# A sign test of 1024 hidden units, done for all of them or, after a bound over 24 token blocks, for the open ones alone

## The chip, the core and the metric

The kernel runs on one core of one Trainium2 chip. The metric is the device time of one execution in microseconds (us). A lower number is better. The chip's TensorE (PE) multiplies matrices, VectorE (DVE), ScalarE (ACT) and GpSimd (POOL) do elementwise work, and SyncE (SP) starts most transfers. Each works off its own list of instructions in order, and they wait for one another by semaphores.

## What is computed

Three layers follow each other. The first is windowed attention with block summaries on 4 x 8 heads of 768 tokens. The second is a soft mixture of experts: 3072 tokens are spread over 32 slots, 8 experts work on 4 slots each, and every token gets a weighted sum of the 32 slot outputs. The third is a top-1 mixture: each token goes through the one expert that its logits choose. Cut to what matters here:

```python
c = np.exp(logits - logits.max(1, keepdims=True))      # combine weights, 3072 x 32
c /= c.sum(1, keepdims=True) + 1e-09
x = c @ slot_out                                       # slot_out is 32 x 512
...
for e in range(E):                                     # 8 experts, top-1
    mask = expert_idx == e
    h = np.maximum(x[mask] @ w1[e], 0.0)               # 1024 hidden units
    out[mask] = gate_w[mask, None] * (h @ w2[e])
```

All tokens of an expert share `u = slot_out @ w1[e]`, which is 32 x 1024: the value of a hidden unit for a token is the product of 32 combine weights and a column of `u`.

## The kernel before

The kernel takes the expert of the first token, loads its weights, and treats all tokens by it first; a loop behind it treats the experts that are then still missing. Within that expert it uses that a unit whose value has the same sign for all tokens needs no `max`: it is zero for all of them or linear in `c`. The linear ones are summed into a 32 x 512 matrix. Only the mixed units have to be computed for each token; up to 96 are allowed (`NPL`), and with the 32 linear rows they fill 128 rows. If there are more, the code of the expert that is treated (`cbx`) becomes zero and the loop at the end does the expert's full product.

The program is in this order.

1. Attention, then the soft mixture (to about 187 us of the profile). Late in it the combine weights are transposed piece by piece into `cT` (`comb_pe`, `comb_ev`, L193 to L201): 128 rows that hold the weights' high and low parts twice, and 3072 columns, one for a token. `first_expert` (L795) chooses the expert and starts the loads of its weights `w1e` and `w2e`.
2. `g_half` and `g_sum` (L984, L998) multiply the slot outputs with `w1e` in two halves of 512 units and sum the parts; `g_parts` (L1001) splits the sum into the high and low rows of `G`. `tok` (L1094) computes logits and norms of the tokens, 128 tokens to a matmul.
3. The sign test: `tile_mm` and `tile_ev` (L1043, L1056), 24 tiles of 128 units by 1024 tokens. Each tile is two matmuls of 512 columns, and its maximum against the sign of the first token is taken while it is read out of PSUM, in turn by ACT and by DVE. Four PSUM areas of two banks are used in the order of the list `order`.
4. `rank` and `places` (L1140, L1168) number the mixed units, make one-hot matrices `OH` of the numbers, collect the columns of these units in `Gm` by matmuls, and fetch their rows of `w2` by an indirect DMA. `lin` (L1122) makes the linear part. Pieces of the norms and codes (`norms`, `codes`) are put between the tiles.
5. The end: `mixed` (L1266) computes the 128 rows for 512 tokens at a time, and 24 groups of three matmuls (L1291 to L1293) write the result `py` of 128 tokens each, which DVE and ACT scale by the gate, and SP writes out. `fill` and the matmuls named `warm` compute nothing that is used.

The order of the work on every engine is that of the code, since the schedule is written by hand; a wait stands where the data need it, and where a PSUM area is used again. In the sign test the main lines are:

```python
for i in range(3 * NU):
    tile_ev(i, tile_mm(i))
    ...
pf = dbank(1, "fill")
fill(6, pf)
rank(6, NU, pf)
places(6, NU, pf)
```

Of the kernel before, what the change touches and what calls it, by code (L numbers as in the profile page):

```python
# [22 lines left out]
P = 128  # L23
# [18 lines left out]
NPL = 96  # L42

# [91 lines left out]
def tile_kernel(ctx, tc, qT, kTd, vwd, phi, w1, w2, emb, tau, u1, u2, consts, consts2, out):  # L135
# [641 lines left out]
    cb = fp.tile([P, 1], F32, name="cb")  # L777
    w1e, w2e = [], []
# [43 lines left out]
    for r in range(2):  # L822
        for fc in range(8):
# [90 lines left out]
    def norms(i):  # L914

        if i == 0:
            for b in range(B):
# [90 lines left out]
    iota = con2[:, C_IOTA : C_IOTA + NPL]  # L1008
    pos = scr[:, 0, 120 : 128]
    ngs = scr[:, 0, 128 : 136]  # L1010
    us = fp.tile([P, NU, 2], F32R, name="us")
    GTf = scr[:, 2, 256:512].rearrange("p (k s) -> p k s", s=NSLOT)
    GNf = hx[:, 3, 256:512].rearrange("p (k s) -> p k s", s=NSLOT)
    GN = w2h[1][:, 0:2, :].rearrange("p a (k x) -> p (a k) x", x=P)
    acc = scr[:, 0, 152 : 176].rearrange("p (k j) -> p k j", j=3)
    fmx = scr[:, 0, 136 : 144]
    flag = fp.tile([P, NU + 1], BF16, name="flag")
    rk = scr[:, 0, 144 : 152]
    idx = fp.tile([P, 1], I32, name="idx")
    OH = w2h[0][:, 0:2, :].rearrange("p a x -> p (a x)")[:, 0 : NU * NPL].rearrange("p (k x) -> p k x", x=NPL)  # L1020
# [3 lines left out]
    junk = [hhi[0].rearrange("p a b -> p (a b)")[:, 0:1024], hlo[0].rearrange("p a b -> p (a b)")[:, 0:1024]]  # L1024
# [6 lines left out]
    with ExitStack() as es:  # L1031
        pst = es.enter_context(tc.tile_pool(name="pst", bufs=1, space=PSUM, reuse_waits="tile"))
        order = [0, 1, 0, 2, 1, 0, 2, 3, 1, 0, 2, 3] + [1, 2, 3] * 4
# [4 lines left out]
        def fill(n, ph):  # L1038

            for _ in range(n):  # L1040
                nc.tensor.matmul(ph[:, 0:512], cTt(0, P), cTt(0, 512), start=True, stop=True)

        def tile_mm(i):  # L1043
# [3 lines left out]
            for c in range(2):  # L1047
                nc.tensor.matmul(  # L1048
                    ph[:, c * 512 : c * 512 + 512],
                    G[:, k * P : (k + 1) * P],  # L1050
                    cTt(1024 * j + 512 * c, 512),
                    start=True,
                    stop=True,
# [3 lines left out]
        def tile_ev(i, ph):  # L1057

            k, j = divmod(i, 3)
            if i % 2 and i != 19:  # L1060
                nc.vector.tensor_tensor_reduce(  # L1061
                    out=junk[1],
                    in0=ph,
                    in1=ngs[:, k : k + 1].to_broadcast([P, 1024]),
                    scale=1.0,
                    scalar=0.0,
                    op0=ALU.mult,
                    op1=ALU.max,
                    accum_out=acc[:, k, j : j + 1],
                )  # L1070
            else:
                nc.scalar.activation(  # L1072
                    junk[0], ph, AF.Relu, scale=ngs[:, k : k + 1], accum_out=acc[:, k, j : j + 1]
                )
# [3 lines left out]
        nc.gpsimd.memset(flag, 0.0)  # L1078
        nc.gpsimd.tensor_copy(us, con2[:, C_U : C_U + NU].unsqueeze(2).to_broadcast([P, NU, 2]))
# [5 lines left out]
        def first(f):  # L1085
            ks = slice(4 * f, 4 * f + 4)
            for k in range(4 * f, 4 * f + 4):
                nc.tensor.matmul(ph0[:, k, :], G[:, k * P : (k + 1) * P], cTt(0, 2), start=True, stop=True)
            nc.vector.tensor_scalar(out=pos[:, ks], in0=ph0[:, ks, 0], scalar1=0.0, scalar2=None, op0=ALU.is_ge)
            nc.vector.tensor_scalar(  # L1090
                out=ngs[:, ks], in0=pos[:, ks], scalar1=-2.0, scalar2=1.0, op0=ALU.mult, op1=ALU.add
            )

# [4 lines left out]
        def kl():  # L1098
            nc.scalar.copy(KL, pk)
            nc.vector.tensor_tensor(out=KL[64:P], in0=pk[64:P], in1=KL[64:P].bitcast(F32), op=ALU.subtract)  # L1100

        def g_cols(k0, k1):
            for k in range(k0, k1):
                nc.tensor.matmul(
                    pgT[:, k, :], pgs[k // 4][:, (k % 4) * P : (k % 4) * P + P], sel[:, 0:NSLOT],
                    start=True, stop=True,
                )
# [4 lines left out]
        def halves(d, name):  # L1112
            t = dbank(d, name)
            return t[:, 0:512], t[:, 512:1024]

        def columns():
            nc.scalar.copy(GTf, pgT)
            nc.gpsimd.tensor_tensor(out=GPT, in0=GTf, in1=pos.unsqueeze(2).to_broadcast([P, NU, NSLOT]), op=ALU.mult)
            nc.gpsimd.tensor_tensor(out=GNf, in0=GTf, in1=ngs.unsqueeze(2).to_broadcast([P, NU, NSLOT]), op=ALU.mult)
            g2 = GNf.unsqueeze(2).to_broadcast([P, NU, 2, NSLOT])  # L1120
            g4 = GN.rearrange("p k (r c s) -> p k r c s", r=2, c=2)
            nc.gpsimd.tensor_copy(g4[:, :, 0], g2)  # L1122
            nc.gpsimd.tensor_tensor(out=g4[:, :, 1], in0=g2, in1=g4[:, :, 0].bitcast(F32), op=ALU.subtract)

# [265 lines left out]
```

## Time and profile before

| | us |
|---|---|
| Median of 3 runs | 259.67 (259.56 to 260.99) |
| Profiled execution | 260.86 |
| Its span, first to last instruction | 259.1 |
| PE busy in it | 236.1 (91%) |
| DVE, ACT, POOL busy | 149.9, 127.3, 91.8 |
| From the end of the slots' sum (187.65) to the first `phm` matmul | 39.9 |
| From there to the first `py` matmul | 4.4 |

The span is what the trace covers; the execution's own time lies 1.76 us above it, and 1.19 us above the median. Times of the trace are counted from the span's start. A matmul of 32-bit data is two records of the trace; PEld is the load of the weights that a matmul holds fixed, which runs beside the matmul before it. The clock column is the granted clock of TensorE: 1.00 is 2.4 GHz, 0.50 is 1.2 GHz, and a value between them is a stretch in which it changed.

### The profile page before, as it was taken

The numbers are of one execution on the slowest core, as the hardware profiler recorded it, in microseconds if no ns is written. First come the engines' busy times: TensorE is split into PE (matmuls) and PEld (weight loads), VectorE is DVE, ScalarE is ACT, GpSimd is POOL, SyncE is SP. The second block draws the span as 40 slices with busy tenths as digits, with TensorE's granted clock in tenths as the row PEclk, the third lists the DMA queues.
The fourth block names the chain that finished last, engine by engine and source line by source line (L and its number), as shares of the span: only waits on it lengthen the run. The fifth ranks groups of instructions, "written<-read, shape, count | busy, mean of one in ns | idle before, by whom it ended". The sixth has DMA issues, their size and how long they took to land.

```text
span 259.1 us, 7977 instructions
## 1 busy us (share of the span) xinstructions
PE 236.1 (91%) x3076; PEld 156.9 (61%) x3076; DVE 149.9 (58%) x697; ACT 127.3 (49%) x291; POOL 91.8 (35%) x131
## 2 busy tenths in 40 slices
PE   6688999989999999999999999998999997879980
PEld 2466877767767778677775433323656844547760
DVE  2547878758778778787855411342115476656840
ACT  1443765657647666467673121423226378434550
POOL 0256577556657665576640100000113540010000
PEclk9979999999999999999999999999999589967997
DMA  6999999999989999955799999997790000014892
GB/s 209 392 411 375 347 331 379 355 367 319 343 306 369 368 326 339 325 226 164 266 339 385 409 397 409 406 408 260 252 385 15 0 0 1 3 30 171 314 399 98
DMA packets 33658, 72.53 MB, mean 280 GB/s; under 512 B 2712, under 2 KB 4504, under 8 KB 33616
## 3 DMA queue, kind: packets, MB, share of 16 engines
q1 hardware_dynamic: 33552, 71.77, 76.0%
q8 instruction: 26, 0.43, 0.6%
q0 software_dynamic: 64, 0.20, 0.3%
q14 instruction: 16, 0.13, 0.1%
HBM read 65.67 MB, written 6.29 MB: 278 GB/s over the span
## 4 chain that ended last, share of the span: by engine, by line
PE 82%; DVE 6%; DMA 2%; issue 2%; ACT 2%; POOL 1%; SPq 1%; POOLq 0%; DVEq 0%; ACTq 0%
PE po L357 11%; PE pt L344 8%; PE s L302 8%; PE pO L831 6%; PE ph L755 6%; PE pv L250 5%; PE tx L390 5%; PE pht L1048 5%; PE lp L408 3%; PE py L1291 3%; DMA fix<-in_kT_dram 2%; PE py L1292 2%; PE pd L262 2%; PE py L1293 2%; PE pa L465 2%
## 5 line engine op out<-in xcount | busy, mean ns | idle before, releaser
L330 POOL TENSOR_TENSOR fix<-fix,nb 128x360 f32<-128x360 f32 x64 | 49.1, 789 | 50.8 <-DVE nb L317 50.6
L317 DVE CUSTOM_DVE_ANT_0 fix<-s,con 128x120 f32<-128x120 f32 x192 | 41.7, 278 | 18.1 <-PE s L302 16.1
L345 ACT COPY pts<-pt 120x384 f32<-120x384 f32 x64 | 27.7, 482 | 13.1 <-PE pt L344 13.1
L336 ACT ACTIVATE fix<-fix 128x360 f32<-128x360 f32 x64 | 29.2, 509 | 7.2 <-POOL fix L330 7.2
L357 PE MATMUL po<-vw,pts 120*64 120x65 f32 x768 | 30.4, 226 | 2.2 <-POOL vw L268 1.0
L357 PEld LDWEIGHTS po<-vw,pts 120*64 120x64 f32 x768 | 25.7, 138 | 8.3 <-issue 2.9
L344 PE MATMUL pt<-con,fix 128*120 128x128 f32 x192 | 28.0, 281 | 1.2 <-ACT fix L336 1.2
L268 POOL COPY vw<-vw 24x780 f32<-24x780 f32 x31 | 26.7, 861 | 2.0 <-POOL fix L330 0.2
L344 PEld LDWEIGHTS pt<-con,fix 128*120 128x120 f32 x192 | 21.4, 140 | 7.4 <-issue 5.0
L1061 DVE CUSTOM_DVE_ANT_0 hlo<-pht,scr 128x1024 fp32r<-128x1024 f32 x11 | 13.3, 1212 | 10.0 <-PE pht L1048 9.9
L374 DVE TENSOR_TENSOR X<-po,den 128x384 f32<-128x384 f32 x32 | 17.8, 557 | 1.1
L400 ACT COPY xT<-tx 128x384 f32<-128x384 f32 x32 | 15.3, 480 | 6.1 <-PE tx L390 5.2
L302 PE MATMUL s<-fix,fix 64*64 64x120 f32 x480 | 17.7, 271 | 0.6 <-DVE nb L317 0.4
L1048 PE MATMUL pht<-cT,gs 128*128 128x512 f32 x48 | 16.8, 478 | 0.6 <-ACT hhi L1072 0.4
L390 PE MATMUL tx<-con,X 128*128 128x128 f32 x96 | 16.4, 282 | 0.0
L1072 ACT ACTIVATE hhi<-pht,scr 128x1024 fp32r<-128x1024 f32 x13 | 14.5, 1116 | 3.9 <-PE pht L1048 3.7
L317 DVE DVE_READ_ACCUMULATOR2_ANT nb<- 128x1 f32 x192 | 16.0, 83 | 0.0
L831 PE MATMUL pO<-w,hx 128*32 128x512 f32 (+1 forms) x152 | 15.4, 509 | 0.0
L278 DVE TENSOR_REDUCE hm<-fix 128x48 f32<-128x768 f32 x16 | 15.1, 944 | 0.4 <-DMA fix<-in_kT_dram 0.4
L302 PEld LDWEIGHTS s<-fix,fix 64*64 64x64 f32 x480 | 12.6, 132 | 4.4 <-issue 3.1
L250 PE MATMUL pv<-vw,con 120*32 120x130 f32 x384 | 15.1, 287 | 0.1
L755 PE MATMUL ph<-w,siT 128*32 128x512 f32 x128 | 14.8, 596 | 0.4 <-DVE siT L578 0.4
(243 smaller groups left out, 356.6 us busy)
## 6 DMA issues: line engine op xcount, KB each, us to landing
w<-in_moe_w_dram SPq DMA_DIRECT2D x30, 1024.0 KB, 10.2
vw<-in_vw_dram SPq DMA_DIRECT2D x32, 390.0 KB, 6.8
fix<-in_kT_dram SPq DMA_DIRECT2D x15, 484.0 KB, 5.4
out_dram<-Y SPq DMA_DIRECT2D x24, 256.0 KB, 2.5
fix<-in_qT_dram SPq DMA_DIRECT2D x15, 384.0 KB, 5.9
w1e<-in_moe_w_dram SPq DMA_DIRECT2D x4, 512.0 KB, 4.4
w2e<-in_moe_w_dram SPq DMA_DIRECT2D x4, 512.0 KB, 8.9
wx<-in_moe_w_dram SPq DMA_DIRECT2D x1, 1024.0 KB, 10.8
```

What stands on the lines that cost most here:

```text
L250: nc.tensor.matmul(pv[32 * g : 32 * g + 32, 0:130], con[:KW, b0 : b0 + 32], vw[:KW, par, x0 : x0 + 130], start=c == 0, stop=c == 2,)
L302: nc.tensor.matmul(sp[j][64 * i : 64 * i + 64, c, :], qns[n % 3][64 * j : 64 * j + 64, 64 * t : 64 * t + 64], kTs[n % 3][64 * j : 64 * j + ...
L317: nc.vector.tensor_tensor_reduce(out=sms[u % 2][:, j, c, :], in0=sp[:, c, :], in1=con[:, m0 : m0 + KW], scale=-0.125, scalar=3.0e38, op0=A ...
L330: nc.gpsimd.tensor_tensor(out=sm, in0=sm, in1=st_["nb", u][:, j].unsqueeze(2).to_broadcast([P, 3, KW]), op=ALU.subtract)
L336: nc.scalar.activation(sm, sm, AF.Exp, scale=-1.0)
L344: nc.tensor.transpose(pt[:, c, :], sms[u % 2][:, j, c, :], ident)
L345: nc.scalar.copy(pts[:, j], pt)
L357: nc.tensor.matmul(po[64 * i : 64 * i + 64, c, j, :], pts[:, j, c, 64 * i : 64 * i + 64], vw[:KW, i, x0 : x0 + 65], start=True, stop=True,)
L390: nc.tensor.transpose(pt[:, c * P : c * P + P], st_["X", b][:, c0 + c, hp * P : hp * P + P], ident)
L755: nc.tensor.matmul(ph[32 * g : 32 * g + 32, :], siT[:, kc, :], w[:, g, :], start=kc == 0, stop=kc == 3)
L831: nc.tensor.matmul(po[c][32 * g : 32 * g + 32, 0 : cs.stop - cs.start], hTs[r][:, fc, 32 * g : 32 * g + 32], w[:, g, cs], start=(r, fc) in ...
L1048: nc.tensor.matmul(ph[:, c * 512 : c * 512 + 512], G[:, k * P : (k + 1) * P], cTt(1024 * j + 512 * c, 512), start=True, stop=True,)
```

## The change

The 24 exact tiles go. In their place there are two levels.

First a bound. The tokens are taken as 24 blocks of 128. While `cT` is made, DVE takes the maximum and the minimum of each of the 32 weights over each block (`box`, 16 reductions), and POOL makes of them a matrix `M` (`box_ends`): a block's midpoints and half widths, with a small slack. A unit's value in a block is at most midpoint times `u` plus half width times `|u|`, so one matmul for 128 units (`bounds`) gives the upper bounds of the unit and of its negative for all blocks, beside the unit's own column. A unit whose bounds leave one sign is settled. The others are called open.

Then the exact test on open units alone. They are numbered in each half of 512 units (`rank1`), at most 128 of a half are collected (`places1`, `candidates`), and 2 x 3 tiles are done as before. The mixed ones among them are numbered again (`rank2`) and collected (`mixed_units`). If a half has over 128 open units or over 96 units are mixed, the full product at the end does the expert (`fits`). The `fill` matmuls go; parts of norms and codes move behind the test.

```diff
+    def box(b, j, bx):
+        v = cTt(b * S, S).bitcast(F32).rearrange("p (g j t) -> p g j t", j=2, t=P)[0:96, :, j, :]
+        for w, op in enumerate((ALU.max, ALU.min)):
+            nc.vector.tensor_reduce(bx[:, w, 6 * b + 3 * j : 6 * b + 3 * j + 3], v, axis=AX.X, op=op)
...
+                late_box = 8 * r + fc in (C_STEPS[4], C_STEPS[5])
+                boxes.append((b, j))
+                if not late_box:
+                    for x in boxes:
+                        box(*x, bx)
+                    boxes.clear()
+                if (b, j) == (B - 1, 1):
+                    box_ends(bx, bm, M)
...
-        order = [0, 1, 0, 2, 1, 0, 2, 3, 1, 0, 2, 3] + [1, 2, 3] * 4
+        order = [1, 3, 2, 1, 3, 2]
...
+        def bound_rows(f):
+            g, pg, h = G[:, f * 512 : f * 512 + 512], pgb[f], slice(NSLOT, 2 * NSLOT)
+            nc.scalar.copy(g[0:64], pg[0:64])
+            nc.scalar.activation(g[64:96], pg[64:96], AF.Abs)
+            nc.vector.tensor_tensor(out=g[h], in0=pg[h], in1=g[h].bitcast(F32), op=ALU.subtract)
+
+        def bounds(f):
+            for k in range(4 * f, 4 * f + 4):
+                nc.tensor.matmul(pub[f][:, k % 4, :], G[0:96, k * P : (k + 1) * P], M, start=True, stop=True)
...
+        def rank1(f):
+            prk = prk1[:, 8 * f : 8 * f + 5]
+            nc.tensor.matmul(prk, ltb, flag1[:, f], start=True, stop=False)
+            for k in range(4):
+                nc.tensor.matmul(
+                    prk[:, k + 1 : 5], oneb, flag1[:, f, k : k + 1].to_broadcast([P, 4 - k]),
+                    start=False, stop=k == 3,
+                )
+
+        def places1(f):
+            ks = slice(4 * f, 4 * f + 4)
+            nc.vector.scalar_tensor_tensor(
+                out=rk[:, ks], in0=prk1[:, 8 * f : 8 * f + 4], scalar=1.0, in1=flag1[:, f, 0:4],
+                op0=ALU.add, op1=ALU.mult,
+            )
             for k in range(4 * f, 4 * f + 4):
...
+                nc.vector.tensor_scalar(
+                    out=OH1[:, k], in0=iota, scalar1=rk[:, k : k + 1], scalar2=ngs[:, k : k + 1],
+                    op0=ALU.is_equal, op1=ALU.mult,
+                )
...
-        for i in range(3 * NU):
-            tile_ev(i, tile_mm(i))
...
-        pf = dbank(1, "fill")
-        fill(6, pf)
-        rank(6, NU, pf)
-        places(6, NU, pf)
...
+        pgs = [g_half(f, A[:, 512 * f : 512 * f + 512]) for f in range(2)]
+        for f in range(2):
+            g_sum(pgs[f], pgb[f])
+        bound_rows(0)
+        bound_rows(1)
         for c in range(4):
             nc.tensor.matmul(pk, soT[:, c, :], SOE[:, c, P - NSLOT :], start=c == 0, stop=c == 3)
         kl()
...
+        bounds(0)
+        bounds(1)
+        flags(0)
+        flags(1)
+        columns(0)
+        columns(1)
+        prk1, pgc = halves(0, "rank1")
+        tok(0, 4)
+        rank1(0)
+        tok(4, 8)
+        rank1(1)
+        tok(8, 12)
         pl_out(0)
...
+        places1(0)
+        tok(12, 20)
+        candidates(0)
+        places1(1)
+        tok(20, 24)
+        pl_out(1)
+        candidates(1)
...
+        for i in range(6):
+            ph = tile_mm(i)
+            tile_ev(i, ph)
+            if i in (3, 5):
+                f = i // 4
+                p = candidates_t(f)
+                nc.scalar.copy(GNc[:, f], p)
+        prk2, pgm = halves(1, "rank2")
+        lin(0)
+        rank2(0)
+        rank2(1)
+        mixed_units()
+        norms(2)
+        fits(cbx, prk2[:, 2:3], NPL, cbs[:, 1:2])
```

Three places show how the instructions move. The first is TensorE behind the slots' sum, before the change: `L988` is `g_half`, `L999` is `g_sum`, `L1096` is `tok`, `L1088` is the sign of the first token, `L1048` are the exact tiles `pht`.

```order
L1211 MATMUL pre_3120<-hx 128x40 x4
L988 MATMUL pre_3118<-w1e_2988,hx 32x512 x2
L988 MATMUL pre_3118<-w1e_2989,hx 32x512 x2
L1096 MATMUL pre_3120<-KL,cT_2868 128x40 x6
L999 MATMUL pre_3119<-scr,con 128x512
L1096 MATMUL pre_3120<-KL,cT_2868 128x40 x6
L1041 MATMUL pre_3118<-cT_2868 128x512 x2
```

After the change the same stretch of TensorE reads so: both halves of `g_half` (`L1017`) and `g_sum` (`L1028`) come first, then `pk` (`L1256`) and the bounds (`L1113`), and `tok` (`L1184`) stands between the numbering (`L1150`) and the collecting of open units (`L1171`).

```order
L1028 MATMUL pre_3154<-scr,con 128x512
L1028 MATMUL pre_3154<-hx,con 128x512
L1256 MATMUL pre_3155<-hx 128x40 x4
L1113 MATMUL pre_3156<-M,gs 128x112 x8
L1184 MATMUL pre_3155<-KL,cT_2868 128x40 x4
L1150 LDWEIGHTS ltb
L1150 MATMUL rank_3208<-flag_3140,ltb 128x5
```

The numbering now follows four matmuls of `tok`, where the exact tiles had begun. A few rows further down TensorE's list goes on like this, up to the first of the tiles that are left.

```order
L1184 MATMUL pre_3155<-KL,cT_2869 128x40 x8
L1171 MATMUL rank_3208<-gs,w2h_3100 128x128 x4
L1184 MATMUL pre_3155<-KL,cT_2869 128x40 x4
L1171 MATMUL rank_3208<-gs,w2h_3100 128x128 x4
L1083 MATMUL pht_3277<-cT_2868,gs 128x512 x2
```

What was matmul work in one piece (tiles of 512 columns beside everything else) is now a row of small matmuls whose inputs come from other engines just before; only 12 matmuls `pht` are left of 48.

The third place is DVE around the choice of the expert, after the change: `L209` are the box reductions, `L866` to `L834` is the chain that chooses the expert, `L876` the copy of its code.

```order
L209 TENSOR_REDUCE bx<-cT_2868 96x3 x6
L866 CAST O_2871<-pO_2870 128x512
L826 COPY x_2872<-px_2984 128x4
L829 TENSOR_REDUCE r_2873<-pl_2985 1x1
L830 SCALAR_TENSOR_TENSOR r_2873<-pl_2985,r_2873,con 1x8
L833 TENSOR_REDUCE r_2873<-r_2873 1x1
L834 TENSOR_SCALAR ei<-r_2873 1x1
L209 TENSOR_REDUCE bx<-cT_2869 96x3 x8
L876 COPY cb<-pcb 128x1
```

Before, nothing stood on DVE between the last `comb_prep` and `L866`'s cast, nor between the choice and the copy of its code. Now eight reductions stand ahead of the one and eight ahead of the other.

## Rows read from the trace of the kernel before

**Rows 1.** Page, first part: span.

```profile
span 259.1 us, 7977 instructions
```

**Rows 2.** Windows: stretch, length, busy us of PE, PEld, DVE, ACT, POOL, clock, DMA.

```profile
187.65:227.50 39.85, 35.72 (x182) 22.90 (x181) 20.72 (x49) 22.78 (x40) 10.05 (x17) 0.91 0.18 67
...
232.00:236.00 4.00, 4.00 (x10) 3.13 (x11) 1.28 (x4) 0.68 (x2) 0.00 (x0) 0.50 0.17 66
236.00:251.50 15.50, 15.49 (x69) 12.18 (x67) 11.55 (x22) 8.38 (x13) 0.00 (x0) 1.00 0.85 325
```

**Rows 3.** Windows of 1 us in which the granted clock changed.

```profile
201.00:202.00 1.00, 1.00 (x9) 1.00 (x9) 0.97 (x3) 0.78 (x2) 0.84 (x3) 0.93 0.00 0
...
208.00:209.00 1.00, 1.00 (x4) 0.83 (x3) 0.75 (x1) 0.66 (x2) 1.00 (x3) 0.66 0.00 0
...
229.00:230.00 1.00, 0.54 (x1) 0.50 (x2) 1.00 (x2) 0.17 (x1) 0.00 (x0) 0.58 0.35 131
...
235.00:236.00 1.00, 1.00 (x4) 0.72 (x3) 0.05 (x1) 0.68 (x2) 0.00 (x0) 0.51 0.68 262
```

**Rows 4.** Chain that ended last: start, us, what.

```profile
187.65 0.70 PE warm L890 x3
...
227.55 0.51 PE phm L1271
...
231.96 0.77 PE py L1291
```

**Rows 5.** Timeline where the boxes go: start, us, engine, line, operation, [idle before].

```profile
172.52 0.48 ACT L198 CAST cT<-pc 128x384 fp32r<-128x384 f32 x1 [0.99 <-PE pc L195]
...
177.97 0.69 DVE L841 CAST O<-pO 128x512 bf16<-128x512 f32 x1 [6.51 <-PE pO L831]
...
185.43 0.16 DVE L851 COPY cb<-pcb 128x1 f32<-128x1 f32 x1 [5.07 <-PE pcb L850]
```

**Rows 6.** Page, costliest groups: busy us, mean ns of one, idle before.

```profile
L278 DVE TENSOR_REDUCE hm<-fix 128x48 f32<-128x768 f32 x16 | 15.1, 944 | 0.4 <-DMA fix<-in_kT_dram 0.4
```

**Rows 7.** Timeline: one half's way from `g_half` to its rows of `G`.

```profile
189.10 1.06 PE L988 MATMUL pre<-w1e,hx 128*32 128x512 f32 x8
...
190.26 0.59 ACT L995 COPY scr<-pre 128x512 f32<-128x512 f32 x1 [0.86 <-PE pre L988]
...
192.68 0.69 DVE L1004 TENSOR_TENSOR gs<-pre,gs 64x512 fp32r<-64x512 f32 x1 [3.04 <-ACT gs L1003]
...
196.24 1.02 PE L999 MATMUL pre<-hx,con 128*128 128x512 f32 x2
```

**Rows 8.** Timeline: small matmuls and weight loads at both clocks.

```profile
190.09 0.85 PE L1096 MATMUL pre<-KL,cT 128*128 128x40 f32 x6
...
200.96 0.99 PEld L1104 LDWEIGHTS pre<-con,scr 128*128 128x128 f32 x8 [0.92 <-DVE scr L1089]
...
202.47 2.04 PEld L1104 LDWEIGHTS pre<-con,hx 128*128 128x128 f32 x8
```

**Rows 9.** Timeline: numbering and one-hot matrix.

```profile
218.11 0.29 PE L1152 MATMUL rank<-flag,oneb 128*128 128x8 bf16 x6
...
225.55 0.36 DVE L1162 TENSOR_TENSOR w2h<-con,scr 128x192 fp32r<-128x192 f32 x1
```

**Rows 10.** Groups, 187 to 232 us: tiles read on ACT and DVE, a small reduction.

```profile
L1072 ACT ACTIVATE hhi<-pht,scr 128x1024 fp32r<-128x1024 f32 x13 | 14.5, 1116 | 3.9 <-PE pht L1048 3.7
L1061 DVE CUSTOM_DVE_ANT_0 hlo<-pht,scr 128x1024 fp32r<-128x1024 f32 x11 | 13.3, 1212 | 10.0 <-PE pht L1048 9.9
...
L1072 ACT ACTIVATION_READ_ACCUMULATOR hhi<-pht,scr 128x1 f32 x13 | 2.5, 192 | 0.0
...
L941 DVE TENSOR_REDUCE scr<-hx 128x24 f32<-128x192 f32 x1 | 0.3, 339 | 0.0
```

**Rows 11.** Timeline: the linear part.

```profile
211.58 1.92 PE L1130 MATMUL lin<-w2e,scr 128*32 128x512 f32 x16
...
214.55 1.05 PE L1137 MATMUL lin<-Y,con 128*32 128x512 f32 x2
```

More of the change, by code (lines that the diff above doesn't have):

```diff
@@ L1032, in tile_kernel, with halves @@
         pst = es.enter_context(tc.tile_pool(name="pst", bufs=1, space=PSUM, reuse_waits="tile"))
-        order = [0, 1, 0, 2, 1, 0, 2, 3, 1, 0, 2, 3] + [1, 2, 3] * 4
+        order = [1, 3, 2, 1, 3, 2]
         def dbank(d, name):
             return pst.tile([P, 1024], F32, tag=f"d{d}", name=name)
-        def fill(n, ph):
-            for _ in range(n):
-                nc.tensor.matmul(ph[:, 0:512], cTt(0, P), cTt(0, 512), start=True, stop=True)
+        def halves(d, name):
+            t = dbank(d, name)
+            return t[:, 0:512], t[:, 512:1024]
         def tile_mm(i):
@@ new lines, in candidates, with candidates_t @@
+        def candidates(f):
+            for k in range(4):
+                nc.tensor.matmul(
+                    pgc[:, f * P : f * P + P], GN[:, 4 * f + k, 0:P], OH1[:, 4 * f + k], start=k == 0, stop=k == 3
+                )
+            (nc.vector.tensor_copy if f else nc.scalar.copy)(Gc[:, f], pgc[:, f * P : f * P + P])
+        def candidates_t(f):
+            p = prk1[:, 32 + f * (P + 2) : 32 + (f + 1) * (P + 2)]
+            for k in range(4):
+                nc.tensor.matmul(p, OH1[:, 4 * f + k], GN[:, 4 * f + k], start=k == 0, stop=k == 3)
+            return p
@@ L1099, in kl @@
             nc.scalar.copy(KL, pk)
[L1100 to L1107, printed above, removed]
+            nc.scalar.copy(pks, pk)
+            nc.gpsimd.tensor_tensor(out=KL[64:P], in0=pks[64:P], in1=KL[64:P].bitcast(F32), op=ALU.subtract)
@@ L1109, in pl_out @@
         def pl_out(h):
             nc.scalar.copy(pl[:, 12 * h : 12 * h + 12], pls[h])
[L1112 to L1123, printed above, removed]
@@ L1140, in rank @@
-        def rank(k0, k1, pf=None):
-            if k0 == 0:
-                st_c["prk"], st_c["pgm"] = halves(0, "rank")
-            prk = st_c["prk"][:, 0 : NU + 1]
-            nc.vector.tensor_reduce(fmx[:, k0:k1], acc[:, k0:k1, :], axis=AX.X, op=ALU.max)
+                st_c["prr"] = halves(0, "lin")[0]
+            prr = st_c["prr"]
+            for k in range(4 * i, 4 * i + 4):
+                g = k % 4
+                nc.tensor.matmul(
+                    prr[32 * g : 32 * g + 32, :], GPT[:, k, :], w2e[k // 4][:, k % 4, :], start=i == 0, stop=i == 1
+                )
@@ new lines, in mixed_units @@
+        def mixed_units():
+            pix = pgm[0:NPL, 128:130]
+            for t in range(2):
+                nc.tensor.matmul(pix, OH2[:, t], GNc[:, t, P : P + 2], start=t == 0, stop=t == 1)
+            nc.vector.tensor_scalar(
+                out=idx[0:NPL], in0=pix[:, 0:1], scalar1=base[0:NPL], scalar2=None, op0=ALU.add
+            )
+            nc.gpsimd.indirect_dma_start(
+                out=wr[0:NPL],
+                out_offset=None,
+                in_=u2.rearrange("e f d -> (e f) d"),
+                in_offset=bass.IndirectOffsetOnAxis(ap=idx[0:NPL, 0:1], axis=0),
+            )
+            for t in range(2):
+                nc.tensor.matmul(pgm[:, 0:NPL], GNc[:, t, 0:P], OH2[:, t], start=t == 0, stop=t == 1)
+            lin(1)
+            nc.vector.tensor_copy(Gm[:, 0:NPL], pgm[:, 0:NPL])
@@ L1276, in mixed @@
         )
-    for i in range(3):
-        mixed(i)
     c = slice(0, 256), slice(256, 512)
+    mixed(0)
+    norms(3)
+    mixed(1)
+    codes(3)
+    prs = bankc(5, "prs")
+    nc.tensor.matmul(prs[NPL:P, :], sel[:, 0:NSLOT], rs, start=True, stop=True)
+    mixed(2)
+    nc.scalar.copy(wr[NPL:P], prs[NPL:P, :])
+    codes(4)
     pw = bankc(6, "warm3")
```

255 lines of the change are left out of this document (103 added, 152 removed).

## The prediction

> **What bounds the kernel now.** I read the windows first, then the chain of waits, then the timeline around the change. The span is 259.1 us [rows 1]. The chain runs through TensorE almost everywhere. Between the end of the slots' sum at 187.65 and the first `phm` matmul at 227.55 [rows 4] lie the sign test and what it needs. There PE is busy 35.7 of 39.85 us, while DVE and ACT have 20.7 and 22.8 and DMA is at 0.18 [rows 2]. This stretch is what the change rebuilds, and nothing of memory bounds it. Then come 4.4 us to the first `py` matmul at 231.96 [rows 4], and the stream of `py` matmuls, where PE is full [rows 2].
>
> The reader must also see the clock. In this execution it leaves 2.4 GHz in the microsecond from 201, comes back in that from 208, leaves again in that from 229 and returns at the end of that from 235 [rows 3]. In the first fall PE was recorded busy all of the microsecond: it issued small matmuls and weight loads. In the second it was busy 0.54 of it. So a busy PE does not keep the clock by itself, and the new stretch, which is made of small matmuls between waits, will not keep it either.
>
> **The change part by part.**
>
> *Boxes.* 16 reductions of 384 elements on DVE. A reduction of 768 takes 944 ns [rows 6], one of 192 takes 339 [rows 10], so 384 lie near 0.54 us, 8.6 us in all. Eight stand ahead of DVE's cast of `O`, which had 6.5 us of idle before it, eight ahead of the copy of the expert's code, which had 5.1 [rows 5]. A pair (1.1 us) is shorter than the 1.47 us between two pieces of `cT` (0.48 and 0.99 [rows 5]). I cost them at nothing. If one took the 944 ns of twice its length, the eight would fill 7.6 us: 1.1 and 2.5 us over their covers, 3.6 us later, with the choice of the expert, its loads and the slots' sum queued behind. POOL's nine small operations for `M` end near 186.5 and are wanted by the bounds 8 us later; `pk` waits for a copy behind them on POOL, with some 6 us of slack.
>
> *Stage 1, to the bounds' rows.* PE starts `g_half` at 188.35, the end of the three warm matmuls (0.70 from 187.65 [rows 4]). The built program makes the second half wait for ACT's copy of the first, and the two halves of `G` wait for each other on one PSUM tile: copy, Abs, subtraction, then again copy, Abs, subtraction. With the prices of one half [rows 7]: 1.06 + 0.59 + 1.06 + 0.59 + 1.0 (second `g_sum`), then twice 0.59 + 0.6 (Abs, as the copy) + 0.69. That is 8.06, and with a dozen hand-overs of 0.05 each 8.65. The rows of the second half stand at 197.0. PE idles over 1 us twice here.
>
> *Stage 2, to the collected open units.* PE works through 4 bounds (the other 4 lie under stage 1), 24 `tok`, 8 collecting matmuls, all with a weight load of 128 columns in front, and two numberings of five small matmuls. At 2.4 GHz a `tok` takes 0.85 / 6 = 0.14 us; at 1.2 the loads double, 8 in 2.04 against 0.99 us [rows 8], so 0.26. 36 of them are 5.0 or 9.4 us. The numberings are 0.6 or 1.0 in all (six such matmuls 0.29 [rows 9]). PE waits for DVE's flags (a reduction of 192, 0.34 [rows 10], and two tiny operations, most of it under `tok`: 0.3), for ACT's copy of the first 12 tokens' tiles, which the built program puts ahead of the thirteenth (0.65, the copy of rows 7), and for the second half's one-hot matrices. Those are four operations of 128 elements, bounded by tiny ones of 0.15 and by the 0.36 of 192 elements [rows 9]; I take 0.25. Behind the last four `tok` they leave 0.9 at 2.4 GHz and 0.4 at 1.2, and a last copy takes 0.3. Sum: 7.6 us at 2.4 GHz, 11.8 at 1.2.
>
> The Trainium skill bears on the one-hot price: "VectorE: DVE Perf Modes", section "The perf-mode tier table", lets `tensor_scalar` on 32-bit SBUF data go at twice the rate of `tensor_tensor`. By an estimate from that the four would end 0.2 us earlier in each half; no row here shows it, and the sum is made without it.
>
> *Stage 3, six tiles.* At 2.4 GHz the readers bound it: three on ACT at 1.12 + 0.19 (DVE's reduction, not in the trace, between 0.94 for 768 and the 1.21 of the older operation on the same tile [rows 6, 10]), two copies of 0.3, the first tile 0.6: 5.1 us. At 1.2 PE bounds it: 12 matmuls at 0.40, eight small ones at 0.26, hand-overs and the last copy 0.8: 7.7 us. 36 of the 48 `pht` matmuls and all of `fill` go, with the readings of 18 tiles, and nothing like them replaces them: that is the gain.
>
> *Stage 4, to `phm`.* Half of `lin` 0.96 [rows 11]; then the second numbering, one-hot, index and columns, some 14 short steps in a chain, PE's 0.05 to 0.2 and DVE's 0.15 to 0.25 with a hand-over each: 2.65; the other half of `lin` 0.96, which stands in front of `phm`; its copy 0.59 [rows 7], for which `phm` waits as it reuses that PSUM area. With hand-overs 5.3 us.
>
> *Behind.* From `phm` to `py` 4.4 us as before [rows 4] plus 0.1: the last matmul of `lin` (1.05 [rows 11]) and its copy move in here, under the reading of `phm`. The norm and code pieces that move here stand on ACT and DVE behind the first `py`'s inputs except one reduction. Gates come about 1 us later than the first `py`; six PSUM areas cover that. The gather of `w2` rows has more room than before.
>
> *The sum.* Stage 1 ends at 197.0. I take the clock to fall near its end and to return in the middle of stage 3, once PE has run `pht` for some microseconds: 11.2 for stage 2 (its start at 2.4 GHz), 6.4 for stage 3, 5.3 for stage 4. `phm` at 219.9 in place of 227.55, `py` 7.5 us earlier. The stream begins at 1.2 GHz as before, where 10 records took 4.0 us against 69 in 15.5 [rows 2]: each microsecond longer at 1.2 costs 0.44. PE does less ahead of it now, so I add 1.5 us of it, 0.7. Gain 6.8 us. The profiled execution took 260.86 and would take 254.1; it lies 1.19 above the median, so the median becomes 252.9.
>
> **Rivals.**
>
> *The clock holds.* If PE keeps 2.4 GHz through stages 2 and 3, `phm` comes at 197.0 + 7.6 + 5.1 + 5.3 = 215.0, 12.5 us earlier: 247.3. For it: the waits are short, none over 2 us. Against it: the fall at 201 with PE busy [rows 3]. Chance 0.17.
>
> *Every burst starts cold.* The clock stays at 1.2 GHz through stage 4 as well, where `lin` then costs 2 us more, and a bound row or hand-over is longer than I have it: 197.0 + 11.8 + 7.7 + 7.3 = 223.8, 3.7 us earlier, less 0.7 for the stream: 256.7. For it: the fall at 229 in a chain of this kind [rows 3]. Against it: the return at 208 while PE still ran such tiles. Chance 0.2. In this direction points the Trainium skill's "TensorE: Matmul & The Clock Gate", section "HAM oscillation": matmul bursts between waits find the clock down each time. By that rule the sum is this rival's; the rows, where the clock came back under `pht`, bear it out only in part.
>
> *The stream loses its clock.* The final stream stays at 1.2 GHz. All its records at that rate would add some 69 x 0.175 = 12 us: 252.9 + 12 = 265. It decides for slower once 39 records more run cold (6.8 / 0.175), 16 us. Against it: the return 4 us after the stream's first matmul [rows 3, 4], under a full PE, which the change leaves as it is. Chance 0.04.
>
> *The test does not hold.* If over 128 units of a half are open, the full product runs and the time is far beyond 300 us: its 24 groups of 24 matmuls at 0.225 [rows 2] alone are 130 us. From the reference's formulas and inputs I count 90 and 81 open units and 58 mixed ones, so chance 0.02.
>
> **How the numbers follow.** The forecast has 0.57, the others 0.17, 0.2, 0.04 and 0.02. Within 0.5% (258.4 to 261.0, about what a measurement tells here from no change) falls the upper tail of the cold rival, 0.03; slower takes the last two less a little, 0.05; faster 0.92. The range takes in most of the two faster rivals, and at the top boxes that overrun their cover: 247.5 to 257.2. It leaves out the far end of the first rival, the slower ones and the far tail of the cold one.
>
> **What would show it.** Box reductions near 0.54 us, DVE's cast of `O` and the copy of the code no later than before. Second rows of `G` near 197. `tok` at 0.26 us with a granted clock of 0.5 for most of 197 to 210, and 1.0 again before `lin`. `phm` near 220 and `py` near 224.5. The forecast is wrong if the clock column stays at 1.0, if `phm` lies past 223, or if the stream's start takes over 6 us at 0.5.

## The result and the profile after

The changed kernel takes 250.2 us (median of 4 runs, 249.72 to 252.55) beside 259.62 us (258.38 to 260.99) for the kernel before: a ratio of 0.9654, 95% interval 0.9575 to 0.9733. Measured again beside the last experiments, it was 251.16 us (6 runs) to 258.38: 0.9705, 0.9651 to 0.9758. A median is over all runs; a ratio leaves out slow runs, those over about 1.5% above the fastest of their kernel. The gain is 7.2 to 9.4 us; the forecast was 6.8 us and 252.9 us. The profiled execution took 249.74 us.

First the span, which answers to [rows 1]:

```profile
span 247.9 us, 7868 instructions
```

The windows that answer to [rows 2], with the same columns: from the point at which [rows 2] begin (the end of the slots' sum) to `phm`, from `phm` to `py`, and the stream of `py`. Below them are four windows of 1 us in which the granted clock changed, as in [rows 3].

```profile
184.70:215.85 31.15, 24.09 (x127) 16.63 (x125) 13.31 (x40) 10.90 (x25) 8.02 (x19) 0.75 0.24 90
215.85:221.60 5.75, 5.07 (x8) 1.87 (x9) 2.91 (x8) 3.00 (x7) 0.51 (x1) 0.56 0.03 9
...
221.60:239.40 17.80, 17.78 (x77) 13.91 (x77) 13.46 (x29) 10.55 (x16) 0.00 (x0) 1.00 0.71 270
```

```profile
193.00:194.00 1.00, 0.00 (x0) 0.00 (x0) 0.47 (x1) 0.78 (x3) 0.05 (x1) 0.80 0.00 0
...
207.00:208.00 1.00, 1.00 (x7) 0.86 (x7) 0.68 (x2) 1.00 (x3) 0.00 (x0) 0.88 0.00 0
214.00:215.00 1.00, 1.00 (x8) 0.00 (x0) 0.96 (x3) 0.00 (x0) 0.63 (x1) 0.54 0.00 0
220.00:221.00 1.00, 0.92 (x3) 0.20 (x1) 0.69 (x2) 0.94 (x3) 0.00 (x0) 0.55 0.00 0
```

Three things are to be seen. The stretch that was rebuilt is no longer full of TensorE work: 24.1 busy us in 31.15, where there were 35.7 in 39.85. It now waits in a chain. The clock is at 1.2 GHz from the microsecond at 193 to that at 207, and again from 214 to the end of 220. And it is back in full just as the stream begins, where before the stream had 4 us at 1.2 GHz in front [rows 2].

Where the 11.1 us between the two spans (259.08 and 247.95 us) went follows from the starts of the same instructions in both traces. `warm` is the run of three warm matmuls at the end of the slots' sum (the expectations call it the second warm run), at 187.41 before and 184.47 after. "Before" and "after" are durations; the last column is the difference.

| stretch | before | after | difference |
|---|---|---|---|
| start of the span to `warm` | 187.41 | 184.47 | -2.94 |
| `warm` to the first tile `pht` | 7.81 | 19.53 | +11.72 |
| first `pht` to `phm` | 32.33 | 11.85 | -20.48 |
| `phm` to `py` | 4.41 | 5.76 | +1.35 |
| `py` to the last copy of `Y` | 19.56 | 17.81 | -1.75 |
| last copy of `Y` to the end | 7.55 | 8.53 | +0.98 |

So from the first tile to `phm` the kernel is 20.5 us shorter (the tiles that went and what stood between them), and the test in their place gave 11.7 us of it back. The first row of the table is not the change's. All of it is there already at earlier warm matmuls, before the change (first line) and after it (second), and the first instruction that the change adds on any engine comes later (third line, after):

```profile
139.77 1.13 PE L598 MATMUL warm<-con 128*128 128x256 f32 x4
...
136.82 1.13 PE L620 MATMUL warm<-con 128*128 128x256 f32 x4
...
146.34 0.22 POOL L215 CAST M<-con 96x48 fp32r<-96x48 f32 x1
```

And of the experiments below, which share the code of that stretch with the changed kernel, some started `warm` at 184.7 to 185.3 us (x3, x6, x8, x9) and others at 187.0 to 187.2 (x2, x4, x5, x7). Without the first row the change is worth 8.2 us in this pair of traces, which lies inside the 7.2 to 9.4 of the medians.

The boxes, in the timeline at the places of [rows 5] (start, us, engine, line, operation, idle before):

```profile
171.57 1.01 DVE L209 TENSOR_REDUCE bx<-cT 96x3 f32<-96x384 f32 x2 [0.16 <-ACT cT L200]
...
173.04 1.01 DVE L209 TENSOR_REDUCE bx<-cT 96x3 f32<-96x384 f32 x2 [0.46 <-ACT cT L200]
...
175.03 0.69 DVE L866 CAST O<-pO 128x512 bf16<-128x512 f32 x1 [0.98 <-PE pO L856]
...
182.49 0.16 DVE L876 COPY cb<-pcb 128x1 f32<-128x1 f32 x1 [0.88 <-PE pcb L875]
```

A reduction takes 0.50 us, and DVE still waits 0.98 us for PE ahead of the cast and 0.88 ahead of the copy: of the covers of 6.51 and 5.07 us the boxes, with their own waits for `cT`, used all but that.

Stage 1 answers to [rows 7]. The bounds are `L1113`; here they wait for DVE's subtraction in each half.

```profile
187.37 1.06 PE L1017 MATMUL pre<-w1e,hx 128*32 128x512 f32 x8 [0.68 <-ACT scr L1024]
...
192.34 0.65 PE L1113 MATMUL pre<-M,gs 96*128 96x112 f32 x4 [1.17 <-DVE gs L1109]
...
193.53 0.68 DVE L1109 TENSOR_TENSOR gs<-pre,gs 32x512 fp32r<-32x512 f32 x1 [1.25 <-ACT gs L1108]
...
194.26 1.10 PE L1113 MATMUL pre<-M,gs 96*128 96x112 f32 x4 [1.27 <-DVE gs L1109]
```

Stages 2 and 3, against [rows 8 to 10]: the weight loads of `tok` at 1.2 GHz, four one-hot operations, and the readings of the tiles (groups of 184 to 217 us; busy us, mean ns of one, idle before).

```profile
199.13 1.78 PEld L1184 LDWEIGHTS pre<-KL,cT 128*128 128x128 f32 x8 [0.76 <-ACT hx L1192]
...
202.56 1.12 DVE L1164 TENSOR_SCALAR gs<-con,rk,scr 128x128 fp32r<-128x128 f32 x4
```

```profile
L1092 DVE TENSOR_REDUCE acc<-pht 128x1 f32<-128x1024 f32 x3 | 3.7, 1225 | 1.1 <-PE pht L1083 1.1
...
L1094 ACT ACTIVATE hhi<-pht 128x1024 fp32r<-128x1024 f32 x3 | 3.1, 1025 | 2.8 <-PE pht L1083 2.8
```

The chain that ended last, behind stage 3, where [rows 4] had 4.4 us from `phm` to `py`:

```profile
213.68 1.51 PE lin L1200 x8
...
215.21 0.59 ACT Y L1204
...
215.85 1.22 PE phm L1308 x2
217.07 1.85 PE prs L1321 x2
218.92 0.74 PE phm L1308
...
220.38 0.54 issue
220.92 0.34 DVE scr L978
...
221.61 0.48 PE py L1338
```

`lin` of the second half stands in front of `phm` and fell into the second drop of the clock (1.53 us against 1.07 for the first half). `prs` in front of `phm` takes 1.85 us, and DVE's `L978` is a piece that the change moved in front of the copy of `w2`.

### The profile page after: what moved, and what is told of

Its sections match the earlier page's. It is cut to its first block, busy times and chain, and to the rows that moved or that the text cites. A ratio compares the mean times of both kernels' runs of the same rounds, so it can differ in the third digit from the quotient of the medians.

```text
span 247.9 us, 7868 instructions
## 1 busy us (share of the span) xinstructions
PE 223.5 (90%) x3021; PEld 148.4 (60%) x3021; DVE 151.0 (61%) x710; ACT 117.8 (47%) x279; POOL 91.6 (37%) x142
## 5 line engine op out<-in xcount | busy, mean ns | idle before, releaser
L366 PE MATMUL pt<-con,fix 128*120 128x128 f32 x192 | 27.3, 277 | 1.4 <-ACT fix L358 1.4
L272 PE MATMUL pv<-vw,con 120*32 120x130 f32 x384 | 14.0, 278 | 0.0
L412 PEld LDWEIGHTS tx<-con,X 128*128 128x128 f32 x96 | 10.7, 141 | 3.7 <-issue 2.8
L324 PE MATMUL s<-fix 64*64 64x120 f32 x288 | 10.8, 272 | 1.1 <-DMA fix<-in_qT_dram 1.0
```

The lines of the kernel that those rows point to most:

```text
L324: nc.tensor.matmul(sp[j][64 * i : 64 * i + 64, c, :], qns[n % 3][64 * j : 64 * j + 64, 64 * t : 64 * t + 64], kTs[n % 3][64 * j : 64 * j + ...
L366: nc.tensor.transpose(pt[:, c, :], sms[u % 2][:, j, c, :], ident)
L412: nc.tensor.transpose(pt[:, c * P : c * P + P], st_["X", b][:, c0 + c, hp * P : hp * P + P], ident)
```

## The experiments

All are edits of the changed kernel. Times are medians. A stretch of two traces is compared from its own start, since the start of `warm` differs by up to 2.9 us between executions of the same code. The same kernel, profiled twice, gave 31.38 and 30.92 us from `warm` to `phm`, and 5.76 and 5.75 from `phm` to `py`: less than half a microsecond is not read from one trace. The ratios of x3 to x7 to the kernel before lie between 0.9590 and 0.9676, and the interval of each overlaps that of the changed kernel: what these five show is read in their traces, by stage.

**x1: the boxes twice** (4 runs).

```diff
                     for x in boxes:
                         box(*x, bx)
+                        box(*x, bx)
```

> Every box reduction is done twice, so 16 more of 0.5 us on DVE, and nothing else changes. Theory (the boxes cost nothing because DVE idles there; with the change 0.98 us of idle are left ahead of the cast of O and 0.88 ahead of the copy of the code): eight more take 4 us, so the cast of O comes some 3.0 us later, and the copies behind the choice another 2 to 3 us later; TensorE waits for both. Slots' sum 5 to 6 us later, time 255 to 256.5. Rival (DVE is off the path by more than that, or the boxes overlap with something that ends later): under 1 us, time 250 to 251.

Measured 253.32 us (252.88 to 253.61), 2.2 to 3.1 us above the changed kernel's two medians and between the two forecasts. In the trace DVE has no idle left ahead of the cast:

```profile
173.59 4.22 DVE L209 TENSOR_REDUCE bx<-cT 96x3 f32<-96x384 f32 x9
...
177.73 0.68 DVE L866 CAST O<-pO 128x512 bf16<-128x512 f32 x1
...
187.41 0.13 DVE L876 COPY cb<-pcb 128x1 f32<-128x1 f32 x1
```

The first copy of `cT` came 0.9 us later than in the changed kernel; counted from it, the cast is 1.8 us late (forecast 3.0), the copy of the code 4.0 (forecast 5 to 6), `warm` 3.3. So the boxes were hidden and twice as many are not: the cover is a real one and it ends. Both sizes were too high. The theory forgot the 0.16 and 0.46 us of idle between the pairs, which swallow some of it.

**x2: the six tiles twice** (4 runs), for what a tile is worth.

```diff
-        order = [1, 3, 2, 1, 3, 2]
+        order = [1, 3, 2] * 4
...
-        for i in range(6):
+        for i in range(12):
```

> Each of the six exact tiles is computed and read twice. Theory (what is saved are tiles, each read out by ACT or DVE in turn, in 1.2 us, or bounded by two matmuls of 0.40 to 0.43 us at the low clock): six more cost 3.7 to 5.2 us, so the 18 removed are worth 11 to 16 us and the bounds' stages have cost most of the difference to the gain; time 254 to 255.5. Rival (tiles were hidden beside other work and the gain is from the removed waits and pieces between them): under 2 us.

Measured 255.35 us (254.43 to 256.22). From the first `pht` to `lin` 9.95 us against 5.95:

```profile
206.65 7.57 PE L1083 MATMUL pht<-cT,gs 128*128 128x512 f32 x20
...
216.60 1.06 PE L1200 MATMUL lin<-w2e,scr 128*32 128x512 f32 x8 [0.62 <-issue]
```

Six tiles are 4.0 us, 0.67 us each, inside the expected 3.7 to 5.2. The 18 that the change took away come to 12 us by that. The rest of the 20.5 would be what went with them or moved ahead of them (`fill`, `tok`, a numbering); no run measures it by itself.

**x3: filling matmuls in stage 1's holes** (4 runs), to keep the clock up.

```diff
+        def fill(n, ph):
+            for _ in range(n):
+                nc.tensor.matmul(ph, cTt(0, P), cTt(0, 512), start=True, stop=True)
...
+        fill(5, A[:, 0:512])
...
+        fill(6, A[:, 0:512])
...
+        fill(3, pgc)
```

> 14 idle matmuls of 512 columns in PE's waits: 5 before and 6 between the two sets of bounds, 3 before the thirteenth tok. Theory (the stretch from the second rows of G to the collected units takes 10 us in place of 7.6, and the tiles 0.6 us more, because the clock is at 1.2 GHz from 193.8 to 207.1): the clock stays at 2.4 through the numbering, phm 2 to 3 us earlier, time 247.5 to 248.5. Rival (the clock goes anyway, as tok and the numbering are small matmuls, or waits bound the stretch): no change within 0.6 us, 249.8 to 251.

Measured 250.85 us (247.46 to 253.71). In the trace the clock fell at 199 instead of 193, with PE recorded busy for 0.70 or more of each of the six microseconds ahead of it, and `warm` to `phm` took 29.8 us:

```profile
199.00:200.00 1.00, 1.00 (x7) 1.00 (x7) 0.00 (x0) 0.00 (x0) 1.00 (x3) 0.55 0.00 0
```

1.6 of the 2 to 3 us expected are in the one trace, and none in the median. That the hole at 193 made the clock fall isn't shown either. The second profile of the unedited kernel has the same hole, at full clock, and its clock fell 2.5 us later, behind two microseconds in which PE was busy for 0.71 and 0.49:

```profile
193.00:194.00 1.00, 0.01 (x1) 0.00 (x0) 0.45 (x1) 0.80 (x3) 0.03 (x1) 1.00 0.00 0
194.00:195.00 1.00, 0.71 (x7) 0.71 (x7) 0.25 (x2) 0.00 (x0) 0.24 (x1) 1.00 0.00 0
195.00:196.00 1.00, 0.49 (x9) 0.39 (x9) 0.86 (x4) 0.00 (x0) 0.43 (x2) 1.00 0.08 16
196.00:197.00 1.00, 1.00 (x15) 1.00 (x13) 0.41 (x3) 0.82 (x3) 0.75 (x5) 0.53 0.00 0
```

**x4: the token products into stage 1's holes** (4 runs).

```diff
-        pgs = [g_half(f, A[:, 512 * f : 512 * f + 512]) for f in range(2)]
+        pgs = [g_half(0, A[:, 0:512])]
+        for c in range(4):
+            nc.tensor.matmul(pk, soT[:, c, :], SOE[:, c, P - NSLOT :], start=c == 0, stop=c == 3)
+        kl()
+        pgs.append(g_half(1, A[:, 512:1024]))
...
+        tok(0, 10)
+        tok(10, 20)
```

> pk and KL are made right after the first g_half, and 20 of the 24 tok run ahead of and between the bounds, where PE waited 1.2 and 1.3 us; the copies of their results follow the columns, and both halves are numbered and collected one after the other. Theory (tok stands on the path between numbering and collecting, at 0.24 us each, and the second half waits for the first one's copy): the first pht 3 to 4 us earlier, phm 3 to 4 us earlier, time 246 to 247.5. Rival (PE does less before the tiles, so the tiles run at 1.2 GHz throughout and give back 1.5 us): time 248 to 249.

Measured 249.87 us (247.64 to 251.72). `warm` to `pht` went from 19.53 to 17.34 us, 2.2 us of the 3 to 4 expected, but the clock came back later in the tiles, and these took 6.90 us instead of 5.95. A second loss stands in the timeline: POOL's work on the tokens' results (`L952`), now early, and the linear columns behind it (`L1143`) lie beside the second four one-hot operations, which take 2.36 us in place of 1.12. In x8 and x9, where the tokens' results are copied for POOL behind the collecting, the same four take 1.12 us again.

```profile
200.38 1.11 DVE L1164 TENSOR_SCALAR gs<-con,rk,scr 128x128 fp32r<-128x128 f32 x4
...
201.42 1.14 POOL L952 TENSOR_TENSOR Y<-hx,ce_all 128x192 f32<-128x192 f32 x2 [0.38 <-ACT hx L1192]
...
201.67 2.36 DVE L1164 TENSOR_SCALAR gs<-con,rk,scr 128x128 fp32r<-128x128 f32 x4
...
202.52 0.73 POOL L1143 TENSOR_TENSOR scr<-w2h 128x256 f32<-128x256 f32 x1
```

**x5: `lin` of the second half between the rank products** (4 runs).

```diff
-            lin(1)
...
         rank2(0)
+        lin(1)
         rank2(1)
```

> Only the place of the sums lin of the second half is changed: from behind the sixteen column products, in front of phm, to between the two rank products, so that phm waits for the row Gm alone. Theory: lin(1) took 1.53 us of the tensor engine's path in the kernel after the change, and phm waits for the engine, so phm comes about 1.6 us earlier counted from the second warm run's start (29.8 us instead of 31.4) and py as much earlier; time about 248.6 us. Rival: the four gates and their row weights, not phm, set when py starts, so phm comes earlier but py and the end don't move (250.2 us, within 0.5 us).

Measured 247.48 us (246.63 to 248.7; ratio to the kernel before 0.9596, 0.9517 to 0.9675). First `lin` to `phm` took 4.31 us instead of 5.90, as expected. Not all of this is the order: x4, in the old order but at full clock up to `phm`, took 5.46, so some 1.15 of the 1.6 us are the order's, and the rest would be the clock's. More came with it: in this execution the clock did not fall at all behind stage 3, and `phm` to `py` took 4.91 us instead of 5.76, with `L978` where it was and `prs` at 1.02 us, which ended before DVE's reading of `phm` did:

```profile
214.00:215.00 1.00, 0.69 (x8) 0.43 (x4) 0.43 (x2) 0.58 (x1) 0.00 (x0) 1.00 0.00 0
216.00:221.00 5.00, 2.92 (x8) 1.11 (x8) 3.97 (x12) 2.91 (x7) 1.25 (x2) 1.00 0.12 39
```

```profile
217.37 1.02 PE L1321 MATMUL prs<-Y,con 128*32 128x512 f32 x2 [0.43 <-DVE cbx L1241]
...
217.93 0.69 DVE L1311 SCALAR_TENSOR_TENSOR hlo<-phm,hhi 128x512 fp32r<-128x512 f32 x1 [0.71 <-ACT hhi L1310]
```

The rival falls: `py` moved with `phm`.

**x6: norms and codes ahead of `phm`** (4 runs).

```diff
-            nc.vector.tensor_reduce(nrm, sq, axis=AX.X, op=ALU.add)
-            nc.vector.tensor_scalar_max(nrm, nrm, 0.0)
+            h = NSLOT // 2
+            while h > 1:
+                nc.gpsimd.tensor_add(sq[:, :, 0:h], sq[:, :, 0:h], sq[:, :, h : 2 * h])
+                h //= 2
...
-        rank2(0)
+        norms(4)
+        rank2(0, lambda: (norms(3), codes(3), codes(5)))
...
+        codes(4)
+        codes(6)
+        row_weights(cbx)
```

> Only the work between phm and the first y is moved: the sum of squares for the norms runs as a tree of additions on POOL before the tiles, instead of as one reduction on the vector engine behind them, and the reciprocals and codes that need no phm are done ahead of it. Theory: phm to py took 5.76 us instead of the 4.41 us before the change because this moved work stands in front of the gates, so the stretch gets 0.4 to 0.9 us shorter, the first y is written about 1.4 us earlier, and the output's tail (last copy of y to the end of the span, 7.8 us) goes back towards 6.9 us: 1 to 1.5 us in all, about 249 us. Rival: py is set by the tensor engine's clock and by its own order, and the tail by the output's transfers, so nothing changes (250.2 us).

Measured 249.44 us (248.0 to 251.97). `phm` to `py` took 5.52 us instead of 5.76, under the expected 0.4 to 0.9 and no more than one trace can tell. The tail was 7.6 us instead of 8.53, but it lies between 7.3 and 8.6 over all traces here, with no order that I can name. The 1 to 1.5 us of the theory did not come. So the moved pieces cost little, and what the 5.76 us have over the forecast was mostly the clock: x5, without the drop, took 4.91.

**x7: the bound rows of the two halves in two PSUM tiles** (4 runs).

```diff
-        pgb = [Bt[:, 512 * f : 512 * f + 512] for f in range(2)]
+        pgb = [Bt[:, 0:512], A[:, 0:512]]
```

> Only a place in PSUM is changed: the bound rows of the second half of the units go to tile A instead of the second half of tile Bt, so that the two halves have no tile in common. Theory: the vector engine's reads of the first half's bounds hold the tensor engine's bounds of the second half back (idle of 1.27 us between them), so the second rows of G come about 0.7 us earlier and phm with them; time about 249.5 us. Rival: the second half waits for its own box products to come through the vector engine, so the idle stays and nothing changes (250.2 us).

Measured 249.28 us (247.34 to 250.69). The second half's bounds start 8.21 us after `warm` instead of 9.79, 1.6 us earlier where 0.7 were expected, and wait 0.55 instead of 1.27 us:

```profile
195.45 0.65 PE L1113 MATMUL pre<-M,gs 96*128 96x112 f32 x4 [0.55 <-DVE gs L1109]
```

`warm` to `phm` is 2.65 us shorter, partly as the clock fell later. But the second drop, which reached from 215 to 225 here, gave 1.55 us back: `py` to the last copy took 19.36 us, not 17.81. The step is as shown; its worth in the end is not told apart from the clock's in one trace.

**x8 to x10: the moves together** (6 runs each). x8 has x4's order (with `pl_out` behind the second `candidates`), x5, x6 and x7; x9 leaves x6 out; x10 leaves x4 out as well.

> All four moves together: the token products right behind the first half's products as in x4_tok_early (but with the two rows pl behind the second half's candidates), lin(1) between the rank products, the bound rows in two tiles, and the norms and codes ahead of phm. Theory: the savings add, since each lies on another step of one chain: from the second warm run's start to phm 31.4 - 2.2 - 0.7 - 1.6 = about 27 us, phm to py about 5, the tail 0.9 shorter; time 244.5 to 247 us. Rival: with fewer products between them the tiles run at 1.2 GHz throughout, and the stream's start too, which gives 1.5 to 2 us back; time 247.5 to 249.5 us.

> x8_all without the moved norms and codes: token products early, two PSUM tiles, lin of the second half between the rank products. Theory: in x8_all the moved reciprocals and POOL's gate product stood inside rank2, where lin to phm took 5.74 us and not the 4.31 us of x5_lin; without them lin to phm is about 4.3 us again, phm comes about 26 us after the second warm run's start and py about 31.3 us after it instead of 33.0: 243 to 243.5 us. Rival: in x8_all the codes taken ahead of phm had paid for that, and without them phm to py grows from 5.49 us by as much: 244.5 to 245 us.

> Of the four moves only two: the two PSUM tiles and lin of the second half between the rank products; the token products stay where the change put them. Theory: the two savings add, as they lie on steps after one another: the second warm run's start to phm 31.4 - 1.6 (the earlier second rows of G) - 1.6 (lin) - 0.4 = about 27.8 us, phm to py 4.9 us, 247 - 1 = about 246 us. Rival: the token products that stand between the rows G's work keep the tensor engine's clock up, so that this order is as good as x9_three, 243 to 244 us.

| | median us (range) | ratio to before, interval | `warm` to `phm` | `lin` to `phm` | `phm` to `py` |
|---|---|---|---|---|---|
| changed kernel, again | 251.16 (249.17 to 251.89) | 0.9705, 0.9651 to 0.9758 | 30.92 | 6.16 | 5.75 |
| x8 | 244.65 (243.9 to 247.68) | 0.9484, 0.9418 to 0.9550 | 27.50 | 5.74 | 5.49 |
| x9 | 245.56 (243.71 to 246.77) | 0.9489, 0.9433 to 0.9544 | 26.50 | 4.31 | 5.70 |
| x10 | 247.67 (246.0 to 249.94) | 0.9562, 0.9504 to 0.9620 | - | - | - |

x8 and x9 beat both kernels: their intervals lie below those of the changed kernel. The savings on the chain to `phm` add, as x8's theory said (27.50 us for "about 27", 244.65 us for 244.5 to 247). x8's own loss stands in its timeline: ahead of the first number `rk` DVE waits for ACT's square root and does two pieces of the norms, so that `rk` starts 1.0 us behind the numbering's matmul, where x9 goes on at once. Then POOL's gate product lies beside the one-hot operation of the chain, and 0.61 us are needed where x9 needs 0.27.

```profile
208.27 0.18 DVE L968 TENSOR_SCALAR scr<-scr 128x24 f32<-128x24 f32 x1 [1.26 <-ACT scr L966]
...
208.84 0.61 DVE L1225 TENSOR_SCALAR gs<-con,rk 128x96 fp32r<-128x96 f32 x1
208.87 0.52 POOL L981 TENSOR_TENSOR hx<-hx,scr 128x192 f32<-128x192 f32 x1 [0.89 <-DVE rk L1222]
```

```profile
208.85 0.27 DVE L1219 TENSOR_SCALAR gs<-con,rk 128x96 fp32r<-128x96 f32 x1
```

x9 has the 1.4 us of its theory from `lin` to `phm`, but not the time: 245.56 us for the 243 to 243.5 forecast, past its rival's 245 too. `py` starts 32.2 us after `warm`, not 31.3, and the tail of this trace is 8.52 us beside x8's 7.35. Which of the two is faster stays open. x10 was forecast at about 246 us and took 247.67. Against x9 it puts the early token products at 2.1 us beside the other two moves; the intervals overlap, but nothing speaks for x10's rival (243 to 244 us). x10's trace is not read here.

**The changed kernel again** (6 runs), for the 2.94 us in front of `warm`.

> The changed kernel as it is, again, beside the two above. Theory: the start of the second warm run at 184.5 us in the one profile of it, 2.9 us earlier than in the kernel before, is a matter of that execution and not of the change, since the code up to there is the same but for the boxes; executions then differ by some 3 us, and the median stays at 249.5 to 250.5 us. Rival: the change moved something in the attention stage for good, and every execution of it starts its second warm run near 184.5 us.

Measured 251.16 us, above the 249.5 to 250.5 expected; its profile, the fastest of its six runs, started `warm` at 184.49 us again. In the two profiles of this kernel alone the rival stands, then. It falls by x2, x4, x5 and x7, where the same code reached `warm` at 187.0 to 187.2, and by the order of the trace: the 2.9 us are complete ahead of the change's first instruction. The six runs point the same way without a profile: two took 249.2 to 249.3 us, the other four 251.1 to 251.9. Part of it comes early: the products `pa` begin at 69.5 us in the first trace of the changed kernel and at 72.1 in x4's. What makes it so I did not find.

## Why the prediction came out as it did

The mechanism held up to `phm`: less work, as a chain at 1.2 GHz, with the clock back in the tiles. All terms of the sum but one lay within 1.3 us of what was measured; that one is the stream, 2.5 us off. Each stage is counted from `warm`.

- *Boxes at nothing*: right. 0.50 us for the 0.54 forecast, 0.98 and 0.88 us of idle left; x1 shows what the cover is worth.
- *Stage 1*, 8.65 us forecast: 8.7 measured (185.52 to 194.21), and the wait of the halves for each other, which the prediction read off the built program, is what x7 took away.
- *Stage 2*, 11.2 forecast: 10.0. The two levels were bracketed (7.6 and 11.8) and the clock was at 1.2 GHz for all of it, so the term for cold work was too dear: a weight load took 0.22 us (1.78 for 8) where I took 0.26 from [rows 8]. The parts that the prediction lists add up to 7.75 and 12.05 us, not to the 7.6 and 11.8 that it gives. The one-hot operations took 0.28 us for the 0.25 taken. The estimate from the Trainium skill's "VectorE: DVE Perf Modes", "The perf-mode tier table", that they would go at twice the rate, is not seen in these 0.28 us.
- *Stage 3*, 6.4 forecast: 5.75. ACT's reading took 1.02 + 0.19 for 1.12 + 0.19, DVE's 1.22, just above the bracket of 0.94 to 1.21, and the clock returned at 207.2, where I had it (the middle of the tiles).
- *Stage 4*, 5.3 forecast: 5.9. The term `lin`, 0.96, was 1.53: the clock fell again in it. This second drop was in the forecast only for the stream, as before the change.
- *`phm` to `py`*, 4.5 forecast: 5.76. The step "4.4 us as before plus 0.1" failed. Before the change the drop from 229.2 to 236.0 lay 2.8 us ahead of `py` and 4.0 behind it; now the drop from 214.1 to 220.9 lies ahead of `py` altogether. In it `prs`, the last matmul of `lin` that was to lie under the reading of `phm`, takes 1.85 us and stands on the chain, and the third `phm` comes behind it; at full clock it took 1.02 us and lay under the reading (x5).
- *The stream*, 0.7 us longer forecast: 1.75 shorter, for the same reason. The drop is as long as before (6.8 us both times), but earlier. x5 (no drop: 4.91 and 17.81 us) and x7 (drop into the stream: 5.76 and 19.36) show both ends of that.

The stages up to `phm` gained 1.1 us more than forecast, the two terms behind it 1.2 us more together, the tail gave 1.0 back: 8.2 us for 6.8. That the total came so close is partly luck, as errors of both signs stand in it: `py` came 37.1 us after `warm` for 37.0 forecast, because stage 2 was as much too dear as the way from `phm` to `py` was too cheap. The rest of the difference of the two profiles is the start of `warm`.

One remark on counting in what stands ahead of the prediction: some matmuls are two records, such as those of `lin` (8 records for 4 matmuls). One of `tok`, `pht` or `py` is a single record, and the prediction counted them so.

Of the rivals, "the clock holds" did not come: the clock stood at 0.75 on the mean up to `phm`. "Every burst starts cold" came half: a second drop in stage 4, but `lin`'s first half at full clock. The prediction named the Trainium skill's "TensorE: Matmul & The Clock Gate", section "HAM oscillation", for it. These traces bear out only that bursts between waits can start at the low level; that the waits are what lowers it they do not show (x3). The stream kept its clock, and the units fitted.

## What to carry to other kernels

When a full stretch of matmuls is replaced by a test with less work, count the test as a chain: its hand-overs, PSUM tiles that two halves share, and work that stands in line without being waited for. Here the test gave back 11.7 of 20.5 us, and moving three such things (x9) returned about 5 of them. Price the path at both clock levels, and ask on which side of each later step a stretch at 1.2 GHz will lie: the same 6.8 us moved cost from the stream to the step ahead of it.

## What was not expected of the hardware

- DVE's `tensor_scalar` took twice its time beside POOL's `tensor_tensor`: four in 2.36 us against 1.11 (x4), one in 0.61 against 0.27 (x8 and x9). Seen twice; no run changes this alone. In x8 the one that needed 0.61 us ended 0.06 us after POOL's, and in x4 each of the four ended 0.08 us after one of POOL's (which end at 202.01, 202.56, 203.25 and 203.95). The Trainium skill's "SBUF — State Buffer", section "SBUF: two separate sides", says of the ports that the two engines share that one of them holds the pair for a whole instruction and the other waits. The ends fit that; which of the two began first the records do not settle, since in x8 DVE's starts 0.03 us ahead of POOL's.
- The granted clock fell with PE recorded busy for 0.70 to 1.00 of each of the six microseconds ahead (x3, at 199), fell in a hole of PE (the first profile of the changed kernel, at 193), and stayed up in the same hole (the second, which fell at 196). The same kernel spent 13.6 us at 1.2 GHz in the first drop of one profile and 10.2 in that of the other, and `warm` to `phm` differed by 0.46 us only.
